# A chunked linear recurrence on one core: the 32-step triangular inverse replaced by two 16-blocks and two sets of matmuls

## The chip, the cores and the metric

One core of one Trainium2 chip. The metric is device microseconds of one execution, median of several; smaller is better.

## What is computed

For each of 4 x 8 = 32 units (batch, head) a 40 x 40 state is carried over 768 steps, and its readings go through a gated mixer:

```python
for t in range(S):                                   # S = 768
    y[:, :, t] = einsum('bhd,bhde->bhe', r_t, state)
    Sa = einsum('bhde,bhe->bhd', state, a_t)
    state = state * w_t[:, :, None, :] - einsum('bhd,bhe->bhde', Sa, b_t)
    state = state + einsum('bhd,bhe->bhde', v_t, k_t)
x = y in (batch, seq, head*dim)                      # 4 x 768 x 320
gate = sigmoid(causal 5-tap convolution of x along seq)
out = (gate * (x @ w_val)) @ w_out
```

All data is float32.

## The kernel before

The 768 steps are cut into 24 **chunks** of 32 steps. Within a chunk the steps depend on each other through a strictly triangular 32 x 32 matrix for each unit; its inverse T replaces the 32 steps by matrix products. So a chunk c has a part that needs no state (**preparation**), and a part that takes the state from chunk c-1 (**recurrence**), and each pair of chunks a **mixer** part.

*Preparation.* `load` brings 838.5 KB (`ew`); `scan` forms running products of the decays (`lam`, VectorE L346); two guard passes `relu` (ScalarE L351, each with an accumulator read) find decays outside a range, in which case the slow general path would run behind; `ln`, `exp` and two Newton passes (L359, L361, L366, L368) form reciprocals; `at` and `kt` (L373, L380) scale the inputs; `qb` (L376) spreads one over a zero-padded tile. `amat` (L385, TensorE) makes two 32 x 32 matrices for each unit; `aev_l` (ScalarE L397) copies one of them to `lst`, `aev_k` and `pre_a` (VectorE L400, L405) make `akb` of the other. `kbt` and `kbe` (L411, L414) transpose the keys. The tiles `qb`, `kbt`, `ak` have NQ = 7 buffers and `lam` NL = 8, so preparation can run up to seven chunks ahead.

*The triangular inverse* is made for a **group** of chunks at once (2 chunks in the first group, then 4, 2 in the last: 7 groups), because 4 chunks x 32 units = 128 matrices fill the 128 partitions, one whole matrix on each. `begin` (L418) transposes `lst` into `x`; then come 30 steps j = 1..30 of two VectorE instructions, `tm = x[j, j+1:] * x[:j, j]` (L426) and `x[:j, j+1:] -= tm` (L429), of j*(31-j) elements for each partition; `diag` (L432) sets the diagonal; `end` (L436) transposes back into `tt`. For each chunk `pre_t` (L441) masks its part into `T`.

*Recurrence* of chunk c, all on TensorE with evacuations between: `u0` (L470, L474) into a PSUM tile `pc`; `evac_u0` (ScalarE L478); `ut` (L483) and `u` (L487), which multiply by T; `evac_ut`, `evac_u` (ScalarE L491, L495); `g` (L499) and its evacuation (VectorE L502); `ysa` and `ysb` (L508) into `pc`; `evac_s`, `evac_y` (VectorE L518, L532), the new state and the output; `st` (L411 on `st`) transposes the state. `load2` and `load3` bring `va`, `w` and `rv`.

*Mixer* for each pair: GpSimd moves the outputs (`xd`, L644) into `xt`, VectorE convolves (L658), ScalarE makes the gate, TensorE multiplies (`val` L89 and L97, `out` L107), GpSimd stores (L707).

*Order.* All this is recorded as operations with an engine, an assumed duration and dependencies. A list scheduler (`Plan.order`) makes one fixed order for each engine from the assumed durations; the engines then follow it, each in order, and wait for each other by semaphores. Results of matmuls outside the recurrence go to NS = 4 PSUM **slots** `pf`, which the scheduler hands out; a slot is free again when the operations named in `give` have read it. Where the plan leaves TensorE idle, it puts dummy matmuls (L726, tile `dm`) to keep the clock up. The mixer's weights are converted from 64-bit data by VectorE at the start (L54 to L61, 5 pieces of 8 instructions).

Of the kernel before, what the change touches and what calls it, by code (L numbers as in the profile page):

```python
# [29 lines left out]
NCST = 292  # L30
NQ, NL = 7, 8
# [232 lines left out]
def fast_path(ctx, tc, ins, out, nch, cst, wts, wz, wmx):  # L264
# [84 lines left out]
    def relu(c, i):  # L349
        wr = st_["ew", c][:, 0:NW].rearrange("p (u t) -> p u t", t=33)[:, :, 1:33]  # L350
        A.activation(out=ern, in_=wr, func=AF.Relu, scale=-1.0 if i else 1.0, bias=bias[:, i:i + 1],  # L351
                     accum_out=wmx[:, c, i:i + 1])

    def recip(c, i):
# [3 lines left out]
        if i == 0:  # L358
            A.activation(out=y0, in_=st_["lam", c][:, :, 1:33], func=AF.Ln)  # L359
        else:  # L360
            A.activation(out=y0, in_=y0, func=AF.Exp, scale=-1.0)  # L361
# [54 lines left out]
    def begin(g):  # L416
        xf = st_["x", g] = ch.tile([128, C, C], F32, name="x", bufs=1)
        V.transpose(out=xf.rearrange("p t s -> p (t s)"), in_=st_["lst", g].rearrange("p i c u -> p (i c u)"))  # L418

    def step(g, j, half):  # L420
        x, n = st_["x", g], 31 - j
        if half == 0:
            st_["tm", g] = wk.tile([128, 240], F32, name="tm")
        tv = st_["tm", g][:, 0:j * n].rearrange("p (s t) -> p s t", t=n)
        if half == 0:
            V.tensor_tensor(out=tv, in0=x[:, j:j + 1, j + 1:32].to_broadcast([128, j, n]),  # L426
                            in1=x[:, 0:j, j:j + 1].to_broadcast([128, j, n]), op=ALU.mult)
# [10 lines left out]
    def pre_t(c):  # L438
        g, c4 = sof[c]
        tm = st_["T", c] = ch.tile([128, 8, C], F32, name="T")  # L440
        V.tensor_tensor(out=tm, in0=st_["tt", g][:, :, c4, :].rearrange("p t u -> p u t"),  # L441
                        in1=maskL.unsqueeze(1).to_broadcast([128, 8, C]), op=ALU.mult)
# [434 lines left out]
```

## Time and profile before

| | before |
|---|---|
| median of 3 runs | 538.73 us (535.99 to 540.53) |
| the profiled execution: time, span | 536.01 us, 533.6 us |
| TensorE busy, share of the span | 422.7 us, 79% |
| VectorE busy | 407.0 us, 76% |
| ScalarE busy | 324.8 us, 61% |
| GpSimd busy | 104.7 us, 20% |
| mean granted TensorE clock | 0.881 |

The span runs from the first instruction to the last; the execution's own time is 2.4 us longer. PE is TensorE's matmuls, PEld its weight loads, DVE VectorE, ACT ScalarE, POOL GpSimd, SP the queue of most loads. Each float32 matmul is two records in the trace, so "x32" is 16 matmuls of the program. A row of a timeline gives start, duration, engine, line, operation, tiles and count, and in brackets the idle time before it with what ended it; "issue" there means that the engine waited for nothing that the profile shows. PEclk is the share of full clock that was granted.

### The profile page before, as it was taken

Reading aid. Unit: us, or ns where it says so; the run is one execution under the profiler, and the core shown is the slowest. Engines: PE = TensorE matmul, PEld = TensorE weight load, DVE = VectorE, ACT = ScalarE, POOL = GpSimd, SP = SyncE. Lnnn points to the kernel's source line nnn. Section 1 sums busy time; section 2 is a strip of 40 time slices with the busy share of each in tenths; the row PEclk is TensorE's granted clock in tenths of the full one; section 3 lists DMA queues with packets and bytes.
Section 4 is the critical chain, followed back from the end, with each engine's and each line's share of the span. In section 5 each row is a group of like instructions: output and inputs, shape, how many; then the busy total and the mean of one; then the engine's idle time right before and its main releaser. Section 6 shows DMA issues by size and latency. Waiting matters only on the chain.

```text
span 533.6 us, 21955 instructions
## 1 busy us (share of the span) xinstructions
PE 422.7 (79%) x9619; PEld 362.8 (68%) x9619; DVE 407.0 (76%) x1026; ACT 324.8 (61%) x652; POOL 104.7 (20%) x188
## 2 busy tenths in 40 slices
PE   5706774973999778797979977999998998899770
PEld 4606673863888667776868776787977786777560
DVE  5549999888899598598896969879998988352330
ACT  3728843762587687478684858867857565543220
POOL 1000000040031032014023140032424041515510
PEclk8767767988799899898797979989998999999967
DMA  8866762173267374437644555644442354401110
GB/s 180 219 150 160 174 162 66 39 168 72 71 151 170 89 173 113 95 76 180 158 96 102 133 109 119 153 112 108 110 103 65 85 121 102 119 11 34 33 20 18
DMA packets 23722, 58.94 MB, mean 110 GB/s; under 512 B 10469, under 2 KB 14603, under 8 KB 21125
## 3 DMA queue, kind: packets, MB, share of 16 engines
q1 hardware_dynamic: 12357, 49.24, 39.8%
q0 software_dynamic: 11264, 8.23, 6.6%
q8 instruction: 77, 1.26, 1.1%
q14 instruction: 24, 0.20, 0.1%
HBM read 49.23 MB, written 3.93 MB: 100 GB/s over the span
## 4 chain that ended last, share of the span: by engine, by line
PE 39%; DVE 19%; DMA 18%; issue 14%; ACT 5%; POOL 4%; SPq 0%; DVEq 0%; POOLq 0%; ACTq 0%
DMA out<-xt 6%; PE pc L508 6%; PE pf L89 5%; PE pf L107 4%; PE pc L487 4%; DMA rv<-in_rv 4%; PE pf L499 4%; POOL xt L644 4%; PE pf L411 4%; DMA va<-in_va 3%; PE pf L385 3%; PE pc L474 3%; DVE x L429 2%; PE pc L470 2%; PE pc L483 2%
## 5 line engine op out<-in xcount | busy, mean ns | idle before, releaser
L644 POOL DMA_DIRECT2D xt<-xe x156 | 82.7, 537 | 222.2 <-DVE tm L426 105.9
L426 DVE TENSOR_TENSOR tm<-x 128x30 f32<-128x30 f32 (+14 forms) x210 | 68.7, 327 | 1.2
L429 DVE TENSOR_TENSOR x<-x,tm 128x30 f32<-128x30 f32 (+14 forms) x210 | 68.6, 326 | 1.0
L658 DVE SCALAR_TENSOR_TENSOR ag<-xt,wts,ag 128x256 f32<-128x256 f32 (+1 forms) x156 | 60.0, 418 | 11.0 <-ACT ag L656 10.9
L707 POOL DMA_DIRECT2D out<-xt x24 | 19.6, 816 | 194.5 <-ACT xt L703 185.7
L726 PE MATMUL pf<-dm 128*128 128x128 f32 x266 | 45.7, 339 | 5.0 <-ACT kbt L414 3.9
L385 PE MATMUL pf<-kb,qb 104*64 104x64 f32 x768 | 31.3, 242 | 21.8 <-DVE x L429 13.4
L726 PEld LDWEIGHTS pf<-dm 128*128 128x128 f32 x266 | 41.8, 246 | 7.1 <-ACT kbt L414 4.6
L351 ACT ACTIVATE er<-ew,bias 104x512 f32<-104x512 f32 x48 | 34.6, 721 | 18.3 <-DVE y L368 9.9
L385 PEld LDWEIGHTS pf<-kb,qb 104*64 104x64 f32 x768 | 28.1, 154 | 25.5 <-ACT er L351 16.6
L107 PE MATMUL pf<-wts,ag 128*128 128x320 f32 x132 | 45.4, 465 | 0.0
L89 PE MATMUL pf<-xt,wts 128*128 128x128 f32 (+1 forms) x208 | 39.0, 317 | 7.4 <-issue 4.3
L483 PE MATMUL pc<-T,ub 64*40 64x32 f32 x1536 | 21.6, 207 | 27.2 <-DVE T L441 12.6
L458 ACT ACTIVATE rb<-rv,cst 104x512 f32<-104x512 f32 x48 | 34.6, 721 | 11.9 <-DMA rv<-in_rv 11.6
L346 DVE TENSOR_TENSOR_SCAN lam<-ew,ind 104x528 f32<-104x528 f32 x24 | 30.1, 1254 | 14.8 <-DMA ew<-in_ew 14.8
L483 PEld LDWEIGHTS pc<-T,ub 64*40 64x40 f32 x1536 | 18.5, 125 | 33.0 <-issue 23.2
L495 ACT COPY w<-pc 32x640 f32<-32x640 f32 x48 | 32.8, 684 | 12.1 <-PE pc L487 11.6
L376 ACT ACTIVATE qb<-qa,cst 104x512 f32<-104x512 f32 x48 | 32.5, 714 | 12.2 <-DVE qa L373 11.0
L89 PEld LDWEIGHTS pf<-xt,wts 128*128 128x128 f32 x208 | 32.9, 225 | 9.2 <-issue 4.7
L487 PE MATMUL pc<-ub,T 64*32 64x80 f32 x768 | 38.2, 258 | 1.0 <-issue 1.0
L411 PE MATMUL pf<-cst,kb 104*128 104x104 f32 x192 | 28.5, 286 | 12.2 <-DVE kb L380 7.4
L508 PE MATMUL pc<-w,kbt 64*40 64x72 f32 x1536 | 33.1, 233 | 5.4 <-issue 4.2
(93 smaller groups left out, 914.0 us busy)
## 6 DMA issues: line engine op xcount, KB each, us to landing
ew<-in_ew SPq DMA_DIRECT2D x24, 838.5 KB
rv<-in_rv SPq DMA_DIRECT2D x24, 624.0 KB
w<-in_vw SPq DMA_DIRECT2D x48, 144.0 KB
va<-in_va SPq DMA_DIRECT2D x24, 160.0 KB
out<-xt POOLq DMA_DIRECT2D x24, 160.0 KB, 7.5
xt<-xe POOLq DMA_DIRECT2D x66, 42.5 KB, 3.5
ag<-in_wts SPq DMA_DIRECT2D x3, 323.0 KB
xt<-in_wts SPq DMA_DIRECT2D x2, 323.0 KB
```

The costliest lines, as they stand in the source:

```text
L89: T.matmul(out=ps[:, j * 2 * L:(j + 1) * 2 * L], lhsT=x[:, m * 128:m * 128 + 128], rhs=xt[:, q:q + 2, 4:4 + L], start=(k == 0), stop=(k == 2))
L107: T.matmul(out=ps, lhsT=gv[r, q * L:q * L + 128], rhs=wo[k][r], start=(k == 0), stop=(k == 2))
L385: T.matmul(out=s[hr(i), j * 64:j * 64 + 64], lhsT=QB[c % NQ][:, pj(j, i)].rearrange("p z t -> p (z t)"), rhs=st_["kb", c][:, pj(j, i)].rea ...
L411: T.transpose(out=s[:, b * 128:b * 128 + ER], in_=src[:, u:u + 2].rearrange("p i f -> p (i f)"), identity=ident[0:ER, 0:ER])
L426: V.tensor_tensor(out=tv, in0=x[:, j:j + 1, j + 1:32].to_broadcast([128, j, n]), in1=x[:, 0:j, j:j + 1].to_broadcast([128, j, n]), op=ALU. ...
L429: V.tensor_tensor(out=x[:, 0:j, j + 1:32], in0=x[:, 0:j, j + 1:32], in1=tv, op=ALU.subtract)
L483: T.matmul(out=PC[0][hr(z, 40), i, j * C:j * C + C], lhsT=UB[hr(i), j, z], rhs=st_["T", c][hr(i), j], start=True, stop=True)
L487: T.matmul(out=PC[1][i * 64 + 32:i * 64 + 64, j // 4, j % 4 * 80:j % 4 * 80 + 80], lhsT=st_["T", c][hr(i), j], rhs=UB[hr(i), j].rearrange( ...
L508: T.matmul(out=PC[g][hr(z, 40), i, j % 4 * 72:j % 4 * 72 + 72], lhsT=l[hr(i, k), j * 2 + z], rhs=rhs[hr(i, k), j * 2 + z], start=start and ...
L644: G.dma_start(out=o, in_=i)
L658: V.scalar_tensor_tensor(out=acc[:, q], in0=xt[:, q, i:i + L], scalar=cw[:, k, i:i + 1], in1=acc[:, q], op0=ALU.mult, op1=ALU.add)
L726: T.matmul(out=PF[i][:, 0:128], lhsT=dm, rhs=dm, start=True, stop=True)
```

## The change

The 32 x 32 triangle is cut into two diagonal blocks of 16 and the block between them.

- `step` works on both diagonal blocks in one instruction: 14 steps j = 1..14 of two instructions with 2*j*(15-j) elements, instead of 30 steps with j*(31-j). `begin` gains a small memset that clears the block between.
- `end2` transposes the upper half of `x` a second time, into `td`.
- The block between is the product of three 16 x 16 blocks. `nblock` and `dblock` (ScalarE, two instructions each for a chunk) spread the block of `lst` and the diagonal block of `td` over zero-padded tiles; `q1` (TensorE, 16 matmuls) multiplies the first with `tt`, `evac_q1` (ScalarE) copies the result, `q2` (TensorE, 16 matmuls) multiplies by the second, and `pre_t` now adds that, from PSUM, to `tt`. One slot is held from `q1` to `pre_t`.
- `aev_l` moves from ScalarE to VectorE and applies a mask (`maskD`), which was `maskL` in `pre_t`; `lst` has two buffers instead of one.
- One of the two guard passes on ScalarE goes; its bound is read from the sum that `exp` accumulates (one more accumulator read there), with one small addition at the end.
- NQ goes from 7 to 6 and NL from 8 to 6.

```diff
-NQ, NL = 7, 8
+NQ, NL = 6, 6
-ACTV = {... "ut": 416, "u": 320, ...}
+ACTV = {... "ut": 416, "q1": 208, "q2": 208, "u": 320, ...}
+    op("nz", "POOL", 4000, [], lambda: [G.memset(x, 0.0) for x in NB + DB + [Q1]])
-    def relu(c, i):
+    def relu(c):
-            A.activation(out=y0, in_=y0, func=AF.Exp, scale=-1.0)
+            A.activation(out=y0, in_=y0, func=AF.Exp, scale=-1.0, accum_out=wmx[:, c, 1:2])
     def aev_l(c, s):
-        A.copy(out=st_["lst", g][:, :, c4, :].rearrange("p i u -> p u i"), in_=s...[:, :, 32:64])
+        V.tensor_tensor(out=st_["lst", g][:, :, c4, :].rearrange("p i u -> p u i"), in0=s...[:, :, 32:64],
+                        in1=maskD.unsqueeze(1).to_broadcast([128, 8, C]), op=ALU.mult)
     def begin(g):
         V.transpose(...)
+        V.memset(x[:, 0:16, 16:32], 0.0)
     def step(g, j, half):
-            V.tensor_tensor(out=tv, in0=x[:, j:j + 1, j + 1:32]..., in1=x[:, 0:j, j:j + 1]..., op=ALU.mult)
+            V.tensor_tensor(out=tv, in0=x[:, :, j:j + 1, j + 1:16]..., in1=x[:, :, 0:j, j:j + 1]..., op=ALU.mult)
+    def end2(g):
+        V.transpose(out=td..., in_=st_["x", g][:, 0:P16]...)
+    def stage_q1(c, s):
+        for j, i in JI:
+            T.matmul(out=s[hr(i), j * 16:j * 16 + 16], lhsT=NB[c % 2][hr(i), j]..., rhs=st_["tt", g][hr(i), P16:C, c4, j], start=True, stop=True)
+    def stage_q2(c, s):
+        for j, i in JI:
+            T.matmul(out=s[hr(i), 128 + j * C:160 + j * C], lhsT=DB[c % 2][hr(i), j]..., rhs=Q1[hr(i), j], start=True, stop=True)
-    def pre_t(c):
-        V.tensor_tensor(out=tm, in0=st_["tt", g][...], in1=maskL..., op=ALU.mult)
+    def pre_t(c, s):
+        V.tensor_tensor(out=tm, in0=s[:, 128:384]..., in1=st_["tt", g][...], op=ALU.add)
-            for j in range(1, 31):
+            for j in range(1, 15):
+        op(nm, "PE", 480, [*B2("nb", c), ("end", g)], ..., give=[("pre_t", c)])
+        op(("evac_q1", c), "ACT", ac(128), [nm, "nz", ("q2", c - 1)], ...)
+        op(("q2", c), "PE", 480, [*B2("db", c), ("evac_q1", c)], ...)
```

Every later line number grows: L385 becomes L388, L411 L415, L470 L501, L474 L505, L483 L514, L487 L518, L499 L530, L508 L539, L726 L766; the two new sets are L461 (`q1`) and L468 (`q2`).

**How instructions stand on VectorE at the end of the first group.** Before, from the last step of the first group to the first chunk's `T` (`tt` is the transpose of `end`, `x<-lst` the next group's `begin`; L57 to L59 convert weights):

```order
L429 TENSOR_TENSOR x<-x,tm 128x30
L58 TENSOR_SCALAR xt<-xt 128x323
L432 MEMSET x 128x32
L58 TENSOR_SCALAR ag<-ag 128x323
L436 STREAM_TRANSPOSE tt<-x 128x1024
L59 SCALAR_TENSOR_TENSOR wts<-xt 128x323
L418 STREAM_TRANSPOSE x<-lst 128x1024
L441 TENSOR_TENSOR T<-tt,cst 128x256
```

The same place in the changed kernel (`td` is the second transpose, `lst<-pf` is `aev_l`):

```order
L437 TENSOR_TENSOR x<-x,tm 128x2x14
L400 TENSOR_TENSOR lst<-pf_117,cst 128x8x32
L440 MEMSET x 128x32
L59 SCALAR_TENSOR_TENSOR wts<-ag 128x323
L444 STREAM_TRANSPOSE tt<-x 128x1024
L448 STREAM_TRANSPOSE td<-x 128x512
L425 STREAM_TRANSPOSE x<-lst 128x1024
L426 MEMSET x 128x16x16
L60 SCALAR_TENSOR_TENSOR ag<-ag 128x323
L473 TENSOR_TENSOR T<-pf_119,tt 128x256
```

The first `T` stands at place 153 of VectorE's order before and at place 92 in the changed one: 32 of the 60 step instructions are gone; the preparation of two chunks and 28 of the conversion's 35 instructions, which stood ahead of it, now stand behind it; six `aev_l`, `td` and two memsets are new ahead of it.

**How they stand on TensorE ahead of chunk 6,** the first chunk of the third group. Before, from `u0` (L470, L474) to `ut` and `u` (L483, L487):

```order
L470 MATMUL pc_112<-va,akb 64x40 x16
L474 MATMUL pc_112<-st,qb_86 64x40 x16
L411 MATMUL pf_114<-cst,st 128x104 x4
L411 MATMUL pf_116<-cst,kb 128x104 x4
L411 MATMUL pf_115<-cst,kb 128x104 x4
L385 MATMUL pf_114<-kb,qb_86 64x64 x16
L483 MATMUL pc_112<-T,ub 40x32 x32
L487 MATMUL pc_113<-ub,T 32x80 x16
```

In the changed kernel, behind `u0` and four rows of `val` (L97 is the rest of `val`, L388 is `amat`, L514 and L518 are `ut` and `u`):

```order
L97 MATMUL pf_119<-xt,wts 64x128 x4
L97 MATMUL pf_119<-xt,wz 64x128 x2
L461 MATMUL pf_117<-tt,nb_103 64x16 x16
L468 MATMUL pf_117<-q_107,db_105 64x32 x16
L461 MATMUL pf_116<-tt,nb_104 64x16 x16
L388 MATMUL pf_118<-kb,qb_84 64x64 x16
L514 MATMUL pc_114<-T,ub 40x32 x32
L518 MATMUL pc_115<-ub,T 32x80 x16
```

The two sets for chunk 6 and the first set for chunk 7 now stand between `u0` and `ut`; `q2` stands directly behind the `q1` whose evacuation it needs, and two of the four slots (117 and 116) are held until the `T` of chunks 6 and 7 are made.

More of the change, by code (lines that the diff above doesn't have):

```diff
@@ L34 @@
 LAT = 180
-ACTV = {"am": 832, "kbt": 338, "g": 832, "u0": 840, "ut": 416, "u": 320, "ysa": 450, "ysb": 720, "st": 275, "val": 1536, "out": 1600}
+ACTV = {"am": 832, "kbt": 338, "g": 832, "u0": 840, "ut": 416, "q1": 208, "q2": 208, "u": 320, "ysa": 450, "ysb": 720, "st": 275, "val": 1536, "out": 1600}
 RHO, CAP, DUM = 0.37, 700, 250
@@ L333, in fast_path @@
     op("ind1", "DVE", 60, ["ind0"], lambda: V.memset(ind[:, :, 0:1], 1.0))
-    op("bias", "DVE", 60, [], lambda: (V.memset(bias[:, 0:1], -WHI), V.memset(bias[:, 1:2], WLO)))
+    op("bias", "DVE", 60, [], lambda: V.memset(bias, -WHI))
     op("pz", "DVE", 1300, [], lambda: (V.memset(PC[0][32:64, :, 0:320], 0.0), V.memset(PC[1][32:64, :, 0:320], 0.0)))
@@ L388, in lz @@
     def lz(g):
-        lst = st_["lst", g] = ch.tile([128, C, 4, 8], F32, name="lst", bufs=1)
+        lst = st_["lst", g] = ch.tile([128, C, 4, 8], F32, name="lst")
         if sg[g][1] < 4:
@@ L552, in fast_path @@
         am = ("am", c)
+        gg = [x for y in range(sg[g - 2][0], sg[g - 1][0]) for x in B2("nb", y)] if g > 1 else []
         if c4 == 0 and sg[g][1] < 4:
-            op(("lz", g), "DVE", 1080, [("begin", g - 1)], lambda g=g: lz(g))
-        op(am, "PE", 870, [("qb", c, 0), ("qb", c, 1), ("kt", c), ("begin", g - 1), ("pre_a", q)], lambda c=c, n=am: amat(c, slot(n)), give=[("aev_l", c), ("aev_k", c)])
-        op(("aev_l", c), "ACT", 604, [am, ("begin", g - 1), ("lz", g)], lambda c=c, n=am: aev_l(c, slot(n)))
+            op(("lz", g), "DVE", 1080, gg, lambda g=g: lz(g))
+        op(am, "PE", 870, [("qb", c, 0), ("qb", c, 1), ("kt", c), ("pre_a", q)] + gg, lambda c=c, n=am: amat(c, slot(n)), give=[("aev_l", c), ("aev_k", c)])
+        op(("aev_l", c), "DVE", 480, [am, "cst", ("lz", g)] + gg, lambda c=c, n=am: aev_l(c, slot(n)))
         op(("aev_k", c), "DVE", 440, [am, ("pre_a", q)], lambda c=c, n=am: aev_k(c, slot(n)))
@@ L563, in fast_path @@
         if c4 == sg[g][1] - 1:
-            op(("begin", g), "DVE", 1140, [("aev_l", x) for x in range(sg[g][0], c + 1)] + [("end", g - 1)], lambda g=g: begin(g))
+            op(("begin", g), "DVE", 1480, [("aev_l", x) for x in range(sg[g][0], c + 1)] + [("end", g - 1)], lambda g=g: begin(g))
             prev = ("begin", g)
-            for j in range(1, 31):
+            for j in range(1, 15):
                 for half in range(2):
                     nm = ("step", g, j, half)
-                    op(nm, "DVE", 70 + j * (31 - j) * 1.04, [prev], lambda g=g, j=j, half=half: step(g, j, half))
+                    op(nm, "DVE", 70 + 2 * j * (15 - j) * 1.04, [prev], lambda g=g, j=j, half=half: step(g, j, half))
                     prev = nm
@@ L573, in fast_path @@
                lambda g=g: end(g))
-        op(("pre_t", c), "DVE", 540, [("end", g), "cst", ("ut", c - 2), ("u", c - 2)], lambda c=c: pre_t(c))
+            op(("end2", g), "DVE", 600, [("diag", g)] + ([y for x in range(sg[g - 1][0], sg[g][0]) for y in B2("db", x)] if g else []),
+               lambda g=g: end2(g))
+        nm = ("q1", c)
+        for z in range(2):
+            op(("nb", c, z), "ACT", ac(128), [("aev_l", c), ("q1", c - 2), "nz", "cst"], lambda c=c, z=z: nblock(c, z))
+            op(("db", c, z), "ACT", ac(128), [("end2", g), ("q2", c - 2), "nz", "cst"], lambda c=c, z=z: dblock(c, z))
+        op(nm, "PE", 480, [*B2("nb", c), ("end", g)], lambda c=c, n=nm: stage_q1(c, slot(n)), give=[("pre_t", c)])
+        op(("evac_q1", c), "ACT", ac(128), [nm, "nz", ("q2", c - 1)], lambda c=c, n=nm: evac_q1(c, slot(n)))
+        op(("q2", c), "PE", 480, [*B2("db", c), ("evac_q1", c)], lambda c=c, n=nm: stage_q2(c, slot(n)))
+        op(("pre_t", c), "DVE", dv(256, 1), [("q2", c), ("end", g), ("ut", c - 2), ("u", c - 2)], lambda c=c, n=nm: pre_t(c, slot(n)))
         op(("load2", c), "SP", 2500, [*B2("ysb", c - 2), ("u0", c - 2)], lambda c=c: load2(c), 2200)
@@ L848, in lay_out @@
     cst[:, 288:290] = own
+    cst[:, 292:294] = own & (i[:, None] >= P16)
     cst[:, 290:292] = (np.arange(128) // 64)[:, None] == np.arange(2)
```

62 lines of the change are left out of this document (39 added, 23 removed).

## Prediction, made before the changed kernel was run

> **What bounds the kernel now.** I read the page's first part, then the busy times of stretches, then the waits, then single places. The page first:
>
> ```profile
> PE 422.7 (79%) x9619; PEld 362.8 (68%) x9619; DVE 407.0 (76%) x1026; ACT 324.8 (61%) x652; POOL 104.7 (20%) x188
> ```
>
> No engine is at its limit on average, but the average mixes three stages. The timeline of TensorE gives where they part: the first `ut` (chunk 0), and that of chunk 2, the first of the second group:
>
> ```profile
> 87.36 1.09 PE L483 MATMUL pc<-T,ub 64*40 64x32 f32 x52 [6.83 <-DVE tm L426]
> 133.97 1.29 PE L483 MATMUL pc<-T,ub 64*40 64x32 f32 x64 [8.86 <-DVE T L441]
> 493.15 0.71 PE L508 MATMUL pc<-w,kbt 64*40 64x72 f32 x32
> ```
>
> TensorE waited 6.83 and 8.86 us there, both times for VectorE, which was in the triangle's steps. The third row is the last `ysb`. The stretches between these points, from the start of the first group's triangle at 35.9 (duration, then busy time by engine, granted clock, DMA):
>
> ```profile
> 35.90:87.40 51.50, 29.77 (x296) 27.00 (x298) 51.37 (x131) 32.34 (x69) 0.00 (x0) 0.73 0.61 148
> 87.40:134.00 46.60, 32.35 (x762) 29.50 (x763) 41.21 (x110) 24.84 (x51) 6.29 (x12) 0.83 0.34 80
> 134.00:493.80 359.80, 323.23 (x8265) 274.05 (x8265) 288.17 (x724) 245.68 (x480) 85.51 (x153) 0.93 0.48 110
> 493.80:533.60 39.80, 20.50 (x144) 16.51 (x139) 9.68 (x38) 7.06 (x24) 10.47 (x16) 0.77 0.11 24
> 376.00:392.00 16.00, 16.00 (x466) 14.49 (x464) 16.00 (x37) 14.23 (x27) 6.99 (x13) 1.00 0.47 105
> ```
>
> So up to 87.4 VectorE is busy all the time (51.37 of 51.5) and sets the end; up to 134 it mostly still does. From 134 to 493.8 **TensorE bounds**: idle for 36.6 us (359.8 - 323.2), and at 0.93 of full clock it loses 7% of the stretch, 25.2 us, to half clock. Its work at full clock is 359.8 - 36.6 - 25.2 = 298.0 us, and 61.8 us are lost. Where nothing is lost (the last row, clock 1.00) it has no gap at all. Who causes the losses there:
>
> ```profile
> PE pc L483 <- DVE T L441: 12.6, 3, 8.9
> PE pc L508 <- issue: 6.8, 5, 2.5
> PE pc L483 <- issue: 6.0, 3, 3.0
> PE pf L385 <- issue: 2.9, 1, 2.9
> PE pc L474 <- issue: 1.9, 2, 1.2
> PE pf L89 <- issue: 1.7, 1, 1.7
> PE pf L385 <- ACT s L414: 1.4, 1, 1.4
> ```
>
> The wait for `T` is 12.6 us, but 8.9 of it is the one that ends at 133.97; only 3.7 us lie inside. More is "issue": 19.3 us in five rows, often in the middle of a set of matmuls, followed by a slower clock:
>
> ```profile
> 214.54 0.23 PE L483 MATMUL pc<-T,ub 64*40 64x32 f32 x2 [3.00 <-issue]
> 214.60:222.00 7.40, 6.50 (x126) 5.92 (x126) 3.04 (x8) 4.71 (x9) 0.00 (x0) 0.77 0.53 119
> 134.00:142.00 8.00, 8.00 (x258) 7.49 (x259) 5.46 (x17) 4.67 (x7) 0.00 (x0) 0.62 0.01 4
> q8 instruction: 77, 1.26, 1.1%
> ```
>
> After that hole of 3.00 us the clock was 0.77 for 7.4 us, 1.7 us lost; after the wait of 8.86 it was 0.62 for 8 us, 3.0 us lost. TensorE's 2 x 9619 records make 250 for each of the 77 packets of the instruction queue; I take the holes for late instruction packets, an inference. The change removes work from VectorE, which bounds the first 134 us, and adds work to TensorE, which bounds the rest.
>
> **The change part by part.** VectorE's prices:
>
> ```profile
> L426 DVE TENSOR_TENSOR tm<-x 128x30 f32<-128x30 f32 x14 | 2.8, 197 | 0.0
> L426 DVE TENSOR_TENSOR tm<-x 128x108 f32<-128x108 f32 x14 | 3.8, 268 | 0.1
> L436 DVE STREAM_TRANSPOSE tt<-x 128x1024 f32<-128x1024 f32 x7 | 13.7, 1956 | 0.0
> L418 DVE STREAM_TRANSPOSE x<-lst 128x1024 f32<-128x1024 f32 x7 | 8.7, 1239 | 0.0
> L688 DVE TENSOR_TENSOR ag<-pf,ag 128x256 f32<-128x256 f32 x22 | 9.3, 423 | 16.4 <-PE pf L89 16.3
> L380 DVE TENSOR_TENSOR kb<-ew,y 104x1024 f32<-104x1024 f32 x24 | 29.3, 1221 | 0.0
> L346 DVE TENSOR_TENSOR_SCAN lam<-ew,ind 104x528 f32<-104x528 f32 x24 | 30.1, 1254 | 14.8 <-DMA ew<-in_ew 14.8
> L366 DVE SCALAR_TENSOR_TENSOR er<-lam,y 104x512 f32<-104x512 f32 x24 | 16.5, 687 | 8.5 <-ACT y L361 8.4
> L57 DVE TENSOR_SCALAR ag<-ag 128x323 int32<-128x323 int32 x3 | 1.0, 331 | 0.0
> L60 DVE SCALAR_TENSOR_TENSOR ag<-ag 128x323 int32<-128x323 int32 x3 | 1.5, 503 | 0.0
> 86.65 0.56 DVE L441 TENSOR_TENSOR T<-tt,cst 128x256 f32<-128x256 f32 x1
> 87.11 0.19 DVE L426 TENSOR_TENSOR tm<-x 128x30 f32<-128x30 f32 x1
> ```
>
> The last two rows show that an instruction starts about 0.1 us before its forerunner ends; I subtract 0.085 us from each duration. 30 elements take 197 ns and 108 take 268, so a step costs 170 + 0.91 n. Before, 60 steps with 2 x 4960 elements are 19.2 - 5.1 = 14.1 us for a group; after, 28 steps with 2 x 1120 elements are 6.8 - 2.4 = 4.4 us: **9.7 us less**. Added for each group: `end2` at half of `begin` (0.6) and a small memset (0.2); for each chunk `aev_l` at the price of L688 (0.34). `pre_t` with a PSUM operand goes from the 0.56 shown to that same 0.42 at most; I cost it at nothing.
>
> *To the first `ut`.* Both orders start the first group's triangle behind the fourth `scan`, so at 35.9. Up to the first `T` VectorE has no gap, so what leaves its order leaves the time: steps 9.7; conversions 20 x 0.25 + 8 x 0.42 = 8.4; preparation that now stands behind (2 `scan`, 3 `er`, 2 `y`, 2 `kb`) 2 x 1.17 + 5 x 0.60 + 2 x 1.14 = 7.6. Added: one `ak` and one `akb` 1.0, four `aev_l` 1.4, `td` 0.6, memsets 0.4. That is 22.3 us less, 64.4 instead of 86.7. Behind `tt` there is now a chain that did not exist: `q1`, a copy on ScalarE, `q2`, then `T`, 1.06 + 0.4 + 1.06 and the semaphores, partly beside `td` and the next `begin`: +3. So `ut` of chunk 0 at **68** instead of 87.4 (65 if the chain is hidden, 75 if TensorE is at half clock and ScalarE, in order, is late).
>
> *Chunks 0 and 1.* VectorE's rows between the first and the third `T` are, at these prices, 24 us (40 before, the same way); TensorE's own chain through two chunks took 15.1 us for chunk 0 (to 102.4) and I take 13 for chunk 1, with the second triangle no longer in the way. So 28 us instead of 46.6 (25 to 33): `ut` of chunk 2 at **96**, 38 us earlier.
>
> *From there to the last `ysb`.* TensorE's prices at full clock, from the chain of waits (start, duration, count):
>
> ```profile
> 368.66 1.06 PE pc L470 x32
> 380.69 1.08 PE pf L385 x32
> 370.78 0.86 PE pf L411 x8
> 421.23 0.75 PE pc L483 x64
> ```
>
> `q1` and `q2` are 16 matmuls each, with 64 x 64 weights in the same two quadrants as L470, and 16 and 32 columns. L470 with 40 columns and L385 with 64 take the same 1.06 and 1.08, so columns don't set it there; **1.06 us a set**. The other end is the rate of L483, 32 matmuls in 0.75, so 0.38 a set; its weights are narrower and use four quadrants, so I stay with L470. Behind `ut` of chunk 2 stand 41 sets: 43.5 us; four `amat` more than before (less was prepared ahead): 4.3; six transposes L411 of 0.43: 2.6; four dummies less: -1. Work 298 + 49 = **347** us.
>
> Of the 61.8 us lost I let VectorE's go: 3.7 waiting and the slow clock behind its waits, 3.0 as shown and by the same measure 1.7 behind each of two later waits: 10.1. Late for it is the new chain: where `q2` stands directly behind its `q1`, TensorE waits about 0.6 for the copy, once for each of five groups, 3. The rest, the holes above all, I leave as it is: 54.7. So this stretch takes 347 + 54.7 = 402 instead of 360.
>
> *ScalarE* loses a guard pass and `aev_l` and gains five small instructions and an accumulator read:
>
> ```profile
> L351 ACT ACTIVATE er<-ew,bias 104x512 f32<-104x512 f32 x48 | 34.6, 721 | 18.3 <-DVE y L368 9.9
> L656 ACT ACTIVATE ag<-xt,wts 128x128 f32<-128x128 f32 x15 | 5.9, 394 | 7.7 <-DMA xt<-xe 7.4 <-DVE ag L688 0.3
> ```
>
> About 0.7 + 0.6 away, 5 x 0.39 in, +0.6 us a chunk on an engine that was busy 246 of 360 us: hidden by TensorE's backlog; uncovered it would be 13 us in 22 chunks. The GpSimd memset runs while the first loads do. The tail, 39.8 us, has none of the changed work.
>
> *Sum.* 96 + 402 + 39.8 = 538 against 533.6, and with the 2.4 us outside the span 540 against 536.0, +0.8%. The median shown is 538.73, 0.5% above the profiled execution; on it this is **542**. A measurement of this kernel can tell about 1% from no change, so the forecast is no change.
>
> [...]
>
> **The rivals.** *R1, faster: the losses were knock-on.* With VectorE relieved, what TensorE needs is ready long before, and more independent matmuls stand in its order; holes then cost their own length and little clock. For: in the stretch quoted with clock 1.00 VectorE was busy 16 of 16 us, so it was close to binding there too. Against: the list names VectorE for 3.7 us only. If 35 us remain instead of 54.7, 518 + 2.4, so 523 on the median.
>
> *R2, slower: slots.* One of the four PSUM slots is held from `q1` to `T`, often two. `amat`, transposes, `g` and the mixer share the rest, and TensorE, in order, stops where a slot isn't read out yet. For: such waits exist with four slots (1.4 for ScalarE's copy of `s`). Against: the order was made with these slots. At 1 us for each of 22 chunks it gives 560 + 2.4, so 565; from about 0.1 us a chunk the result is over 1% slower.
>
> **How the numbers follow.** The forecast has 0.40, R1 0.32, R2 0.28. The forecast's own range is 531 to 552: the start 65 to 75, the two chunks 25 to 33. Sets at L483's rate would take 28 us off, into R1's land. To leave out no more than 2 in 10 the range goes to R1 and R2: 518 to 565. Faster by over 1%: R1 and a little, 0.34. Within 1%: 0.30. Slower: R2 and the forecast's upper part, 0.36.
>
> **What would show it.** `ut` of chunk 0 near 68 and of chunk 2 near 96; L461 and L468 near 1.06 us for 32 records at full clock; VectorE well under TensorE from then on; idle "issue" time near 20 us and clock near 0.93 in the long stretch. Wrong would be a set that takes half as long, waits of pf sets for slots over 5 us, or a clock over 0.97.

## The result, and the profile after

The changed kernel took **568.93 us** (median of four executions, 564.45 to 577.15), the kernel before 538.83 beside it: ratio 1.054, 95% interval 1.045 to 1.062. The forecast was 542 with a range of 518 to 565; it was wrong, and the kernel is slower. Executions of one kernel here spread over some per cent (twelve of the kernel before, in experiment 10, took 524.66 to 543.03 us): a median is over all of a run's executions, a ratio with its interval only over those within 1.5% of the fastest. The profiled execution is the slowest of the four (577.15 us, span 575.3); profiled again on another chip, the same kernel took 573.0 us with the same shape.

From the page, the busy times and the queue of instruction packets:

```profile
PE 485.4 (84%) x11043; PEld 420.1 (73%) x11043; DVE 356.4 (62%) x840; ACT 340.2 (59%) x724; POOL 106.8 (19%) x193
...
q8 instruction: 88, 1.44, 1.1%
```

VectorE has given up 50 us of busy time and TensorE has taken on 63. The three marks on TensorE's timeline (first `ut`, `ut` of chunk 2, last `ysb`):

```profile
73.05 1.17 PE L514 MATMUL pc<-T,ub 64*40 64x32 f32 x57 [0.83 <-DVE T L473]
103.42 1.26 PE L514 MATMUL pc<-T,ub 64*40 64x32 f32 x60
534.96 0.71 PE L539 MATMUL pc<-w,kbt 64*40 64x72 f32 x32
```

TensorE's wait for `T` is 0.83 us at the first mark and gone at the second (6.83 and 8.86 before). The stretches between the marks (duration, then busy time by engine, granted clock, DMA), the long one first:

```profile
103.20:535.70 432.50, 393.18 (x9729) 339.05 (x9727) 279.64 (x653) 282.61 (x593) 91.94 (x165) 0.88 0.43 100
35.90:73.05 37.15, 25.23 (x282) 21.71 (x283) 31.33 (x72) 23.50 (x52) 0.00 (x0) 0.59 0.60 143
73.05:103.20 30.15, 27.31 (x754) 25.37 (x756) 24.04 (x71) 16.34 (x34) 0.00 (x0) 0.78 0.32 79
535.70:575.30 39.60, 21.47 (x139) 16.82 (x139) 6.92 (x26) 5.93 (x21) 10.29 (x16) 0.71 0.11 24
```

| stretch | before | forecast | after |
|---|---|---|---|
| to the first `ut` | 51.5 | 32 | 37.15 |
| to `ut` of chunk 2 | 46.6 | 28 | 30.15 |
| to the last `ysb` | 359.8 | 402 | 432.5 |
| of it: TensorE's work at full clock | 298.0 | 347 | 341.3 |
| of it: idle | 36.6 | | 39.3 |
| of it: lost to half clock | 25.2 | | 51.9 |
| of it: the two losses together | 61.8 | 54.7 | 91.2 |
| tail | 39.8 | 39.8 | 39.6 |

The losses are made as in the prediction: idle is 432.5 - 393.18, and 12% of 432.5 is lost at a clock of 0.88; a clock given to two digits leaves 2 us open in the work and in the loss. The start gained 30.8 us, not quite the 38 forecast. In the long stretch the work is what was forecast, and idle time is nearly what it was. **What came on top is the clock: 26.7 us more lost.** The waits inside the long stretch show that it does not come from waits for other engines:

```profile
PE pc L514 <- issue: 13.4, 8, 3.8
PE pc L539 <- issue: 8.4, 7, 3.5
PE pf L530 <- ACT kbt L418: 4.5, 1, 4.5
PE pf L530 <- issue: 3.5, 3, 2.6
PE pf L468 <- issue: 2.0, 2, 1.8
PE pf L530 <- ACT s L418: 1.4, 1, 1.4
```

VectorE's waits are 1.3 us in all (15.0 before, 8.9 of them the one that ends where the stretch begins). "Issue" is 29.4 us in all its rows (20.9 before); waits for a slot to be read out by ScalarE (L418 in these rows) are about 7 us (4 before).

The prediction took the "issue" holes for late instruction packets, as an inference. The times of the packets in the traces bear it out: in the profiles of the two kernels, 27 of the 28 "issue" holes of more than 0.6 us (14 of 15 before, 13 of 13 after) end 1.2 to 1.75 us after an instruction packet has landed; of moments taken at random in the same two profiles 8% do. But the packets went up by 14% (88 instead of 77) and "issue" by 41%, and the second profile of the same kernel has 24.1 us of it, so the number of packets alone doesn't give the time.

A slow spell is now much longer than the hole ahead of it. TensorE's timeline of one of the two longest (start, duration):

```profile
353.75 0.47 PE L539 MATMUL pc<-w,kbt 64*40 64x72 f32 x17 [2.19 <-issue]
354.14 3.54 PE L107 MATMUL pf<-wts,ag 128*128 128x320 f32 x6
357.62 1.92 PE L468 MATMUL pf<-q,db 64*64 64x32 f32 x32
359.34 1.91 PE L501 MATMUL pc<-va,akb 64*64 64x40 f32 x32
361.18 1.93 PE L505 MATMUL pc<-st,qb 104*64 104x40 f32 x32
363.05 3.87 PE L107 MATMUL pf<-wts,ag 128*128 128x320 f32 x6
366.84 1.65 PE L415 MATMUL pf<-cst,st 104*128 104x104 f32 x8
368.42 1.29 PE L514 MATMUL pc<-T,ub 64*40 64x32 f32 x64
...
371.78 1.15 PE L388 MATMUL pf<-kb,qb 104*64 104x64 f32 x32
```

and the busy times there and behind it:

```profile
354.10:368.40 14.30, 14.30 (x124) 9.75 (x116) 6.91 (x14) 4.86 (x10) 0.93 (x2) 0.51 0.32 72
371.00:380.00 9.00, 9.00 (x276) 8.31 (x274) 7.27 (x12) 7.39 (x17) 4.36 (x9) 0.97 0.31 75
```

A hole of 2.19 us, and then 14.3 us without any gap at a clock of 0.51: `q2` (L468) takes 1.72 us there until the next set starts, against 1.05 at full clock. The clock record goes back to 1.00 at 371.57, behind `ut` (L514, from 368.42) and during `u` (L518, 80 columns, from 369.64). In both profiles the clock record has the values 1.0 and 0.5 alone, and changes at multiples of 3.41 us; call such a piece a window (before 117 at 1.0 and 38 at 0.5, after 110 and 57). In the long stretch of before, no window at half clock in which TensorE was over 90% busy was followed by another at half clock; in the changed kernel 12 were. The clock falls about as often as before, but it stays down longer: 10 spells with 14 windows at half clock before, 13 spells with 31 windows after (11 with 30 in the second profile).

### The profile page after: what moved, and what is told of

Read it like the earlier page. It is cut to its first block, busy times and chain, and to the rows that moved or that the text cites. A ratio compares the mean times of both kernels' runs of the same rounds, so it can differ in the third digit from the quotient of the medians.

```text
span 575.3 us, 24726 instructions
## 1 busy us (share of the span) xinstructions
PE 485.4 (84%) x11043; PEld 420.1 (73%) x11043; DVE 356.4 (62%) x840; ACT 340.2 (59%) x724; POOL 106.8 (19%) x193
## 3 DMA queue, kind: packets, MB, share of 16 engines
q1 hardware_dynamic: 12357, 49.24, 35.9%
## 4 chain that ended last, share of the span: by engine, by line
PE 66%; DMA 10%; issue 9%; DVE 8%; ACT 5%; POOL 1%; SPq 1%; DVEq 0%; POOLq 0%; ACTq 0%
PE pc L539 9%; PE pf L107 7%; PE pc L518 6%; PE pf L89 6%; PE pf L415 6%; PE pf L468 5%; PE pf L530 5%; PE pf L461 5%; PE pf L388 4%; PE pc L501 4%; PE pc L514 4%; PE pc L505 4%; DMA w<-in_vw 3%; DMA ew<-in_ew 3%; DMA out<-xt 2%
## 5 line engine op out<-in xcount | busy, mean ns | idle before, releaser
L684 POOL DMA_DIRECT2D xt<-xe x156 | 82.7, 536 | 189.9 <-DVE xt L60 106.6
L107 PE MATMUL pf<-wts,ag 128*128 128x320 f32 x132 | 51.0, 511 | 0.0
L415 PE MATMUL pf<-cst,kb 104*128 104x104 f32 x192 | 28.4, 288 | 24.1 <-DVE kb L383 13.8
L415 PEld LDWEIGHTS pf<-cst,kb 104*128 104x128 f32 x192 | 21.4, 159 | 27.7 <-DVE kb L383 14.0
L530 PE MATMUL pf<-rb,vu 104*64 104x64 f32 x768 | 32.3, 243 | 9.4 <-ACT kbt L418 4.5
L539 PE MATMUL pc<-w,kbt 64*40 64x72 f32 x1536 | 36.2, 240 | 3.8 <-issue 3.8
L518 PE MATMUL pc<-ub,T 64*32 64x80 f32 x768 | 38.5, 260 | 0.9 <-issue 0.9
L514 PE MATMUL pc<-T,ub 64*40 64x32 f32 x1536 | 25.2, 215 | 15.8 <-issue 13.4
L530 PEld LDWEIGHTS pf<-rb,vu 104*64 104x64 f32 x768 | 28.6, 155 | 13.5 <-issue 4.8
L539 PE MATMUL pc<-re,s 40*40 40x72 f32 x1472 | 34.5, 239 | 4.6 <-issue 4.6
L728 DVE TENSOR_TENSOR ag<-pf,ag 128x256 f32<-128x256 f32 (+2 forms) x39 | 13.8, 358 | 39.4 <-PE pf L89 25.4
L107 PEld LDWEIGHTS pf<-wts,ag 128*128 128x128 f32 x132 | 23.6, 207 | 17.5 <-issue 10.9
L514 PEld LDWEIGHTS pc<-T,ub 64*40 64x40 f32 x1536 | 21.5, 132 | 19.8 <-issue 16.1
L539 PEld LDWEIGHTS pc<-w,kbt 64*40 64x40 f32 x1536 | 30.9, 124 | 6.7 <-issue 6.3
L388 PE MATMUL pf<-kb,qb 104*64 104x64 f32 x768 | 34.5, 257 | 1.0 <-DVE kb L383 0.5
```

What stands on the lines that cost most here:

```text
L107: T.matmul(out=ps, lhsT=gv[r, q * L:q * L + 128], rhs=wo[k][r], start=(k == 0), stop=(k == 2))
L388: T.matmul(out=s[hr(i), j * 64:j * 64 + 64], lhsT=QB[c % NQ][:, pj(j, i)].rearrange("p z t -> p (z t)"), rhs=st_["kb", c][:, pj(j, i)].rea ...
L415: T.transpose(out=s[:, b * 128:b * 128 + ER], in_=src[:, u:u + 2].rearrange("p i f -> p (i f)"), identity=ident[0:ER, 0:ER])
L514: T.matmul(out=PC[0][hr(z, 40), i, j * C:j * C + C], lhsT=UB[hr(i), j, z], rhs=st_["T", c][hr(i), j], start=True, stop=True)
L518: T.matmul(out=PC[1][i * 64 + 32:i * 64 + 64, j // 4, j % 4 * 80:j % 4 * 80 + 80], lhsT=st_["T", c][hr(i), j], rhs=UB[hr(i), j].rearrange( ...
L530: T.matmul(out=s[hr(i), j * 64:j * 64 + 64], lhsT=st_["vu", c][:, pj(j, i)].rearrange("p x t -> p (x t)"), rhs=st_["rb", c][:, pj(j, i)].r ...
```

## The experiments

The theories, numbered as the expectations name them. **A**: the granted clock follows what the array streams, not whether TensorE has gaps; the new sets stream 16 and 32 columns for each weight load and so keep it low. **B**: more instructions, more holes, each with its own slow clock. **P**: the planner assumes 480 ns for a set of 1.06 us, so its order is bad. **D**: the shorter run-ahead (NQ, the prepared chunks; NL, the decay tiles). **L**: any change of the order moves the time. **W**: what is left is the sets' TensorE time alone. B and A are the two first thoughts; the others are rivals to both. Where an edit is made to the kernel before, the text says so; the others start from the changed kernel.

**1. Wider streams.** Each matmul of both sets streams 64 columns, by repeating its own:

```diff
-  out=s[.., j*16:j*16+16],       rhs=tt[.., P16:C, c4, j]
+  out=s[.., j*64:j*64+64],       rhs=tt[.., P16:C, c4, j].unsqueeze(1).to_broadcast([64, 4, P16])
-  out=s[.., 128+j*C:160+j*C],    rhs=Q1[.., j]
+  out=s[.., j*64:j*64+64],       rhs=Q1[.., j].unsqueeze(1).to_broadcast([64, 2, C])
```

> The changed kernel, with both new sets streaming 64 columns a matmul (the same 16 or 32 columns repeated) instead of 16 and 32; the same number of matmuls and weight loads, and a set of 64 columns took 1.10 to 1.15 us in the profile of the changed kernel against 1.06 to 1.11 for the new ones. Theory A (the granted clock falls because the new sets feed the array few columns for each weight load): the clock of the long stretch goes from 0.88 back to 0.92 or more, its half-clock spells of 17 us go, and the time falls by 15 to 27 us, to 542 to 554. Theory B (the loss comes from more holes in the instruction stream, each with its own half-clock aftermath, because there are 3072 more instructions): the time stays within 1% of 569, or rises by up to 4 us for the longer streams.

559.47 us (554.84 to 564.59), ratio 1.044, interval 1.035 to 1.052. Neither A's range nor B's. The profile has the clock A wanted, 0.94 in the long stretch, and another price that A had not seen:

```profile
104.62:522.92 418.30, 382.25 (x9729) 330.66 (x9725) 280.05 (x652) 283.34 (x593) 92.25 (x165) 0.94 0.44 104
```

One `q1` on its timeline:

```profile
227.91 1.96 PE L461 MATMUL pf<-tt,nb 64*64 64x64 f32 x32
```

`q1` reads its columns from `tt` with a stride of 32 elements; 64 of them took 1.89 us from one set to the next instead of 1.04, while the 64 contiguous columns of `q2` took 1.08. That is 24 x 0.85 = 20 us of added work. (The columns of `q1` are also repeated four times and those of `q2` twice; no run separates the stride from that.)

**2. Thin sets.** Two of the 16 matmuls of each set are left.

```diff
-        for j, i in JI:
+        for j, i in JI[:2]:
```

> The changed kernel with 2 of the 16 matmuls in each new set, whose results are copied over all blocks (the output is then not the reference's); plan, waits, slots and copies stay. It takes away 42 matmuls' worth of 48 sets: 48 x 7/8 x 1.06 us = 44.5 us of TensorE work. If the new sets cost their work alone, the time goes from 569 to about 525 (520 to 530). If they also brought the extra loss of the long stretch, by clock (A) or by holes (B), 91 us lost there against 54.7 before, it falls further, to 488 to 505. If another chain (VectorE, the waits for the new copies) is close behind, it stays above 530.

523.3 us (522.25 to 524.35), ratio 0.979, interval 0.973 to 0.984: 45.6 us less, as their work alone. But the parts are not those of that reading:

```profile
96.81:482.15 385.34, 337.83 (x8573) 286.31 (x8573) 278.55 (x653) 280.50 (x594) 92.23 (x165) 0.93 0.48 112
```

The clock is back at 0.93 (27 us lost), the work is 310.8 us, and idle time is up to 47.5. So with an eighth of the sets' price the change gains 2.1%, some 12 us, although its start is 37 us shorter there (60.9 us to `ut` of chunk 2, 98.1 before): the long stretch takes back 5 us for the rest of the sets, 7 of work that the kernel before does under its long start, 11 of idle time and 2 of clock.

**3. The planner's price.** 1060 ns instead of 480 for `q1` and `q2`.

```diff
-        op(nm, "PE", 480, [*B2("nb", c), ("end", g)], ...
+        op(nm, "PE", 1060, [*B2("nb", c), ("end", g)], ...      # and the same for q2
```

> The changed kernel with the planner told 1060 ns for each new set instead of 480 (they took 1.06 to 1.11 us): only the order and the number of filler matmuls change. Theory P (the plan is wrong by 48 x 0.58 = 28 us of TensorE time, so its order makes TensorE wait): 545 to 560, less idle time by waits. Theories A and B: within 1% of 569, since the holes named issue and the clock loss do not come from the order.

574.59 us (565.11 to 582.80), ratio 1.063, interval 1.051 to 1.075. P falls. Another order has the same loss (clock 0.88, idle 44.5):

```profile
103.82:535.39 431.57, 387.05 (x9707) 335.02 (x9705) 278.65 (x644) 281.87 (x590) 92.26 (x165) 0.88 0.43 99
```

**4. Run-ahead, in the kernel before.** First both cut to six, then one at a time, and the load buffers from three to two as a control.

```diff
-NQ, NL = 7, 8
+NQ, NL = 6, 6        # then 7, 6 and 6, 8
```

```diff
-        ew = ld.tile([ER, EWF], F32, name="ew", bufs=3)      # the control
+        ew = ld.tile([ER, EWF], F32, name="ew", bufs=2)
```

> The kernel before with six prepared chunks and six decay tiles (of seven and eight); nothing else. Theory D (the shorter run-ahead costs the long stretch its cover): 550 to 565. A and B: within 1% of 538.8.

> The kernel before with seven prepared chunks and only the decay tiles cut from eight to six. With both cut to six the kernel before took 583.5 us instead of 535.7. Theory D-chunks (the prepared chunks carry the loss): within 1.5% of 536. Theory D-decay (the decay tiles hold back the scan, with which each chunk's preparation begins): 570 to 590. Theory L (any change of the plan's order can cost tens of us, and the run-ahead is not it): anywhere, with no order among the cuts.

> The kernel before with six prepared chunks and eight decay tiles. D-chunks: 570 to 590. D-decay: within 1.5% of 536. L: anywhere.

> The kernel before with two buffers for the loads of a chunk's decays, keys and removal vectors instead of three: the control for the next run, which needs this space. Loads are then issued one chunk later. If loads are not on the path, within 1.5% of 536; if they are, a few us more, all at the start, where DMA is busiest (0.61 of the time up to 87 us).

Medians, with that of the unchanged kernel on the same chip: 583.52 (535.70) for 6 and 6; 578.39 (541.65) for 7 and 6; 552.99 (541.65) for 6 and 8; 552.33 (541.65) for two load buffers. So the decay tiles are dear in the kernel before, 37 us, and chunks cost 11, as much as the control, which was to cost little. With both at six, idle time in the long stretch is twice that of before, and the clock is low too:

```profile
102.45:540.56 438.11, 364.11 (x8471) 307.32 (x8471) 330.91 (x790) 269.17 (x527) 91.89 (x165) 0.87 0.43 100
```

In that stretch TensorE waits 27.5 us for VectorE (6.0 before, without the wait at its edge), 18.7 for ScalarE (9.2) and 28 for "issue" (21). The longest three:

```profile
PE pc L508 <- DVE w L502: 11.3, 3, 7.8
PE pc L508 <- issue: 9.0, 8, 4.1
PE pc L483 <- ACT ub L478: 8.6, 9, 4.5
```

**5. Run-ahead, in the changed kernel.** Seven chunks with two load buffers; then seven decay tiles, with one buffer for `db`.

```diff
-NQ, NL = 6, 6
+NQ, NL = 7, 6        # "ew" with two buffers; then 6, 7 with one "db"
```

> The changed kernel with seven prepared chunks instead of six, the space for it taken from the load buffers (two instead of three), everything else as in the changed kernel. D-chunks: the loss of the long stretch goes back from 91 us to about 55, so 530 to 545. D-decay (decay tiles still six), A and B: within 1.5% of 569, plus what the control shows. L: anywhere.

> The changed kernel with seven decay tiles instead of six, the space taken from the second buffer of the diagonal block's weights. In the kernel before, cutting eight decay tiles to six cost about 37 us and cutting seven chunks to six about 11. Theory D-decay for the changed kernel too: 545 to 560. If its triangle is short enough that TensorE does not wait for the run-ahead (waits for other engines in the long stretch are some 10 us in all): within 1.5% of 569.

584.96 us (575.29 to 595.63; before 541.65) and 574.68 (563.18 to 580.10; before 533.51). Neither helps. D, which costs the kernel before more than the whole change does (48 against 30 us), is not shown for the changed one by these two: each had a buffer taken elsewhere, and only a clear gain would have spoken for it.

**6. Wider streams without the strided price.** `q1` 32 columns, `q2` 64; then with seven decay tiles.

```diff
+  out=s[.., j*32:j*32+32],       rhs=tt[.., P16:C, c4, j].unsqueeze(1).to_broadcast([64, 2, P16])
+  out=s[.., j*64:j*64+64],       rhs=Q1[.., j].unsqueeze(1).to_broadcast([64, 2, C])
```

> The changed kernel with the first new set streaming 32 columns (its 16 twice) and the second 64 (its 32 twice); count and order of instructions as in the changed kernel. In the run that streamed 64 in both, the first set took 1.89 us at full clock instead of 1.04, 24 x 0.85 = 20.4 us of added TensorE time, while the second stayed at 1.08; 32 columns of the first should stay near 1.05. Theory A (a 3.41 us window in which TensorE streams too few columns, weighted with the rows in use, is followed by a window at half clock): the time loses the 20 us and keeps the better clock, so 539 to 548, granted clock 0.87 or more. Theory B (more holes): 565 to 572, granted clock 0.83 to 0.85 as in the changed kernel.

> Both of the last two together. If A and D-decay are separate and both true: 525 to 535, faster than the kernel before. If only A: 539 to 548; if only D-decay: 545 to 560.

555.06 us (550.87 to 564.76), ratio 1.035, interval 1.022 to 1.047; and 561.10, ratio 1.050, interval 1.041 to 1.058. About half of what A expected, and nothing from the decay tiles. The profile of the first is as A said: same work (344.8 us) and idle time (37.2), clock 0.93.

```profile
101.18:511.96 410.78, 373.55 (x9731) 323.10 (x9727) 280.34 (x653) 282.25 (x593) 91.89 (x165) 0.93 0.44 106
```

**7. The guard pass alone.** The kernel before without its second `relu` pass.

```diff
-        op(("relu1", c), "ACT", 720, [("relu0", c)], lambda c=c: relu(c, 1))
-            A.activation(out=y0, in_=y0, func=AF.Exp, scale=-1.0)
+            A.activation(out=y0, in_=y0, func=AF.Exp, scale=-1.0, accum_out=wmx[:, c, 1:2])
```

> The kernel before with one guard pass less (the second bound read from the sum that the exponential leaves), nothing else of the change: 24 ScalarE passes of 0.72 us go and 24 short reads come. ScalarE is busy 0.58 of the span before, and TensorE waits for it some 10 us in all: within 1% of 538 in every theory of the loss; more than 10 us either way would mean that a change of order alone moves this kernel as far as the edits do (theory L).

543.72 us (532.09 to 548.48) against 533.51 (529.12 to 540.55): the medians differ by 10 us, with 15 us less of ScalarE's busy time (310.1 against 324.8). That is L's sign, just reached, but not clear of noise: the ranges overlap, and one of the four executions is as fast as the kernel before. The control of experiment 4 is clear (all four above all seven of the kernel before), but it also holds back the loads. So L is suggested, not shown.

**8. Changed kernel and wider copy on one chip, five rounds.**

> The changed kernel as it is, again, on the same chip as the next run. Ratio 1.045 to 1.065 against the kernel before, granted clock 0.83 to 0.85.

> The copy that streams 32 and 64 columns, again. Theory A: faster than the run beside it by more than their spread, by 10 us (the medians so far) to 21 us (the clock loss that the two profiles differ by), granted clock 0.86 or more. If the earlier difference was one of chips: within 1% of the run beside it.

569.03 us (560.58 to 573.02), ratio 1.053, interval 1.045 to 1.062, against 567.49 (558.74 to 574.16), ratio 1.048, interval 1.041 to 1.056. A's expectation missed and the other came true: the two can't be told apart in time, so most of the earlier difference was not one of the columns. The mean granted clock of the six executions is 0.849 and 0.862, as A said, but this time the profile of the wide copy has long spells too. The changed kernel, then the wide copy:

```profile
102.65:531.53 428.88, 393.29 (x9729) 338.82 (x9727) 280.64 (x652) 282.60 (x593) 91.87 (x165) 0.88 0.43 101
102.09:533.08 430.99, 388.14 (x9729) 333.33 (x9727) 280.51 (x653) 283.14 (x593) 91.90 (x165) 0.89 0.43 101
```

Windows at half clock with TensorE busy that were followed by another at half clock: 15 here in the changed kernel, 13 in the wide copy, but 2 in the wide copy's profile of experiment 6. One profile of a kernel doesn't fix how long its slow spells are.

**9. Two levels for the first six chunks only.** The kernel before with its NQ and NL, the new triangle and sets for groups 0 and 1; then with the guard pass away.

```diff
+TWO = 2
+            for j in range(1, 15 if g < TWO else 31):
+    NB = [QT[6][:, 8 * i:8 * i + 8] for i in range(2)]   # the seventh chunk's buffers
```

> The kernel before, with the two-level triangle (and the wider streams) for the first two groups, chunks 0 to 5, and the triangle of 30 steps for the other five groups; seven prepared chunks and eight decay tiles as before. The weights of the new sets stand in the buffers of the seventh chunk, which is prepared later for it. Theory W: the start falls by some 30 us (98 to 66 us for the two stages up to the third chunk), of which 17 us come back as work that the long stretch then has to do, and 12 sets of 1.05 us, 13 us, are paid: 535 - 30 + 17 + 9 (4 chunks' sets in the long stretch) = 531, range 520 to 540. Theories D and L: the run-ahead is cut for the seventh chunk, or the order is a worse one: 540 to 560.

> The same with one guard pass less. By the ScalarE time alone no more than 3 us from the run beside it; a difference of 8 us or more would again be one of order, as the guard pass alone moved the kernel before from 534 to 544.

542.27 us (539.21 to 552.52), ratio 1.010, interval 1.004 to 1.016; 547.54 (543.90 to 554.83), ratio 1.019, interval 1.014 to 1.025. W's 531, with its range to 540, was missed on the side of D and L; the step between the two, 5 us, lies between what ScalarE's time and what L would make of it. In the profile of the first (its slowest execution, 552.52) the start to chunk 2 is 82.7 us (98.1 before), 15 us less and not the 30 that W counted on, and the long stretch takes it back, with idle time of 51.1 and clock 0.91:

```profile
81.07:118.55 37.48, 32.54 (x852) 30.29 (x852) 27.57 (x73) 23.64 (x51) 4.88 (x10) 0.74 0.30 77
118.55:510.60 392.05, 340.95 (x8489) 289.12 (x8489) 299.41 (x751) 257.47 (x515) 87.05 (x156) 0.91 0.46 107
```

No version that does all the work was faster than the kernel before.

**10. The suspect doubled.** Each new set issued twice, narrow and wide, on one chip.

```diff
-        for j, i in JI:
+        for j, i in JI + JI:
```

> The changed kernel with the 16 matmuls of each new set issued twice over, to the same place: 48 x 1.05 us = 50.4 us of TensorE time more, from 569. Theory A, the new sets' few columns as a cause of the clock loss: the loss grows with them, so 569 + 50 + 10 to 25 = 629 to 645, granted clock 0.83 or less. If the clock loss does not hang on the new sets: 614 to 624, at a granted clock of 0.85 or more.

> The same with 32 and 64 streamed columns. The sets took 1.04 and 1.08 us against 1.04 and 1.05, so the TensorE time is the same to 48 x 0.015 = 0.7 us. Theory A: 612 to 622, at least 12 us below the run beside it, granted clock 0.87 or more. Otherwise: within 4 us of the run beside it.

621.66 us (618.08 to 634.58), ratio 1.175, interval 1.166 to 1.184, against 606.46 (598.60 to 614.60), ratio 1.138, interval 1.124 to 1.151. All six wide executions are faster than all six narrow ones, at a mean clock of 0.876 against 0.830. Both totals are 6 to 7 us under A's ranges; the narrow one, taken alone, lies in the range of the other reading, though at A's clock. (On this chip the kernel before took 533.55 us, 538.83 beside the changed one.) The difference, which doesn't hang on the chip, is A's: **15.2 us** by the medians, 20 by the ratios. The long stretches, narrow and wide:

```profile
113.56:586.10 472.54, 436.59 (x11041) 384.59 (x11039) 278.27 (x645) 283.19 (x593) 91.95 (x165) 0.88 0.39 92
108.98:559.03 450.05, 412.91 (x11043) 361.92 (x11039) 278.69 (x648) 282.64 (x593) 91.92 (x165) 0.93 0.41 97
```

Idle is 36.0 and 37.1 us, work at full clock 380 and 381, and only the clock differs: 57 and 32 us lost. The instructions, their order and the idle time are the same; what differs is the columns (and the layout of the two results): with doubled sets, the narrow streams had the lower clock, 0.88 against 0.93.

## Why the prediction was wrong

**The start: size nearly right.** `ut` of chunk 0 came at 73.05 (forecast 68, in its range to 75), the next stretch took 30.15 (28). Three things make up the 5 us. The triangle began at 37.40 instead of 35.9. VectorE, forecast without a gap, waited 3.4 us in three places for `amat` (L388), the longest shown first. And the two sets behind `tt` ran at a clock of 0.50 (67.8 to 73.05), which the forecast had kept for its upper end: 1.9 us each, not 1.06:

```profile
50.69 0.61 DVE L400 TENSOR_TENSOR lst<-pf,cst 128x256 f32<-128x256 f32 x1 [2.27 <-PE pf L388]
67.97 1.89 PE L461 MATMUL pf<-tt,nb 64*64 64x16 f32 x32 [0.51 <-DVE tt L444]
70.30 1.92 PE L468 MATMUL pf<-q,db 64*64 64x32 f32 x32 [0.45 <-ACT q L464]
```

The small copies, too, were dearer than costed, by less than 1 us up to there:

```profile
L400 DVE TENSOR_TENSOR lst<-pf,cst 128x256 f32<-128x256 f32 x24 | 14.4, 602 | 15.1 <-PE pf L388 15.1
L473 DVE TENSOR_TENSOR T<-pf,tt 128x256 f32<-128x256 f32 x24 | 14.3, 595 | 26.9 <-PE pf L468 24.6 <-ACT rb L489 1.3 <-ACT ub L509 1.0
L452 ACT ACTIVATE nb<-lst,cst 128x128 f32<-128x128 f32 x48 | 22.4, 513 | 13.2 <-DVE lst L400 13.2
```

`aev_l` and `pre_t` were costed at 0.42 and took 0.60, `nblock` at 0.39 and took 0.51: the rows of before that stood for them read and write in other patterns. Which operand makes the difference wasn't measured.

**TensorE's added work and its price: right.** A set was to take 1.06 us; from its start to the next set's it took 1.04 (`q1`) and 1.05 (`q2`) at full clock, in the median, and the work is 341.3 us against 347. (The last step of the forecast's sum, 540 raised by 0.5%, gives 543, not 542.)

**The step that failed is "The rest, the holes above all, I leave as it is: 54.7".** It was 91.2. In the profiled execution the span missed the sum of 538 by 37 us: 7 at the start, 36.5 here, less 6 of work. VectorE's waits did go; idle time stayed, because "issue" rose by 8.5 us, to 29.4; and the clock lost 26.7 us more. I took the clock loss for something that follows a hole and ends by itself. The holes did not become many more; the spells behind them became longer, 2.4 windows instead of 1.4, and 17 more windows at half clock are 29 us. In the two profiles, what TensorE streamed in a window goes with the clock of the next. For each window inside the two long stretches the streamed columns of all matmul records that start in it are added up, each weighted with its rows as a share of 128; the medians, with the number of windows and the range:

| window, next window | before | after |
|---|---|---|
| full clock, full clock | 3502 (81; 1936 to 5712) | 3392 (83; 1692 to 5560) |
| full clock, half clock | 1600 (9; 512 to 2286) | 1386 (12; 0 to 2096) |
| half clock, full clock | 2007 (10; 1496 to 3081) | 2288 (13; 1280 to 3152) |
| half clock, half clock | 2005 (4; 1534 to 2388) | 1544 (18; 528 to 2816) |

The ranges overlap, and at half clock the medians differ in the changed kernel alone; this is what two profiles show, not a test. TensorE's busy time does not set the 18 apart: it was over 90% busy in 12 of them.

The spell quoted above lies with the 18: from 354.14 to 368.42 its records come to 6068, or 1450 in 3.41 us (a third of L107's matmuls use 64 rows); `ut` behind it comes to 1024 in 1.22 us, or 2865. The same sum can be made for the sets, an estimate from their columns and times in this profile. At full clock `q1` (256 in 1.04 us) has 840 in 3.41 us and `q2` (512 in 1.05) 1660, half or less of the 3392 of the windows that stayed there. At half clock the mixer's L107 has about 1500, `u0` 1190 (L501) and 1900 (L505) and the transposes L415 1460, less than the 2288 of the windows with full clock behind them. Those are in both kernels. So A is only part: in that spell, wide columns for `q2` would have raised 1450 to 1573, still near the 1544. In the 12 windows that prolonged a slow spell with TensorE busy, the new sets fill 11 of 41 us, `out` and `val` 12, `u0` 4.

How much of the miss is the narrow streams? Doubled, they cost 15.2 us, so singly about half, 7.6, an estimate (10 by the ratios); the direct comparisons gave 1.5 us on one chip and ratios 1.9% apart on two. That is a quarter to a third of the 27 us by which the median missed the forecast. The start's 7 us are another quarter. The mean clock was 0.845 over ten executions of the changed kernel, 0.862 over ten of the wide copy and 0.871 before; the means mix the stages, and the start, which is slow in all three, is shorter in two. What the wide copy leaves of the lower clock shows in its second profile, and the changed kernel's shows with another order too; it isn't traced to one edit. The run-ahead is suspected, since its cut lowers the clock of the kernel before to 0.84. But the thin sets (experiment 2) and the doubled wide ones (experiment 10) kept six and six and had 0.93 in the long stretch, and with wide streams a seventh decay tile brought nothing. What the cut costs in the changed kernel, and where half of the miss comes from, stays **open**.

**The rivals.** R1 (losses are knock-on and go with VectorE's waits) fails in the changed kernel. R2 (slots) had the right sign and the wrong mechanism: waits for a slot were about 7 us, 3 more than before, not 22 more; that is over the 5 us that the prediction named as a sign of being wrong. The change of NQ and NL was in the diff. The prediction counted the preparation that it moves behind the start, but gave the shorter run-ahead itself no price; in the kernel before it costs 48 us, and nothing in a profile of one run-ahead would have priced it.

## What to carry to other kernels

Moving work to TensorE had two prices here, the time of its instructions and what they did to the clock of all others: a set of 16 matmuls took 1.04 us with 16 columns, 1.05 with 32 and 1.08 with 64 contiguous ones, but with the sets doubled the mean clock was 0.830 with the few columns and 0.876 with twice as many. When the start of a pipeline is shortened, look for the work that was done under it: of 37 us gained, 12 were left even with the new sets all but free. And where two load buffers instead of three already move a statically ordered kernel by 2%, a change that promises less can't be judged from its own arithmetic.

## What was not expected of the hardware

- Half clock with TensorE 100% busy for 14.3 us (0.51 from 354.10 to 368.40). In the changed kernel's long stretch the 18 windows at half clock with another behind them had streamed 1544 columns in the median, weighted by rows, the 13 with full clock behind them 2288.
- TensorE's holes that no semaphore explains, 0.62 to 4.33 us long in the two profiles, ended 1.2 to 1.75 us after an instruction packet had landed (27 of 28).
- With a moving operand read with a stride of 32 elements, 16 and 32 columns (16 repeated twice) took the same 1.04 us a set, 64 (16 repeated four times) 1.89; contiguous, 64 (32 repeated twice) took 1.08.
- ScalarE's passes over 128 elements for each partition took 0.51 us in `nblock`, which reads with a stride and scales, and 0.26 in `evac_q1`, a plain copy out of PSUM:

```profile
L464 ACT COPY q<-pf 128x128 f32<-128x128 f32 x24 | 6.3, 262 | 19.3 <-PE pf L461 16.9 <-PE pf L468 2.4
```
